# Shift of the maxima in two 64-row tiles, product with v in four 32-column tiles by key tile, and all work in the order of a fixed table

## The chip, the cores and the metric

The kernel runs on one core of a Trainium2 chip. Its engines are TensorE (PE in the profile, its weight loads PEld), VectorE (DVE), ScalarE (ACT), GpSimd (POOL) and SyncE (SP), which issues nearly all DMAs. The metric is the device time of one execution in microseconds (us).

## The reference

Attention with a hash mask over four batches of eight heads, 768 positions and 64 dimensions, and behind it a gated MLP. Cut to what matters:

```python
mask = q_bucket[:, :, :, None] == k_bucket[:, :, None, :]
scores = scale * np.matmul(q, k.transpose(0, 1, 3, 2))
scores = np.where(mask, scores, -1000000000.0)
scores = scores - np.max(scores, axis=-1, keepdims=True)
attn = np.exp(scores)
attn = attn / (np.sum(attn, axis=-1, keepdims=True) + 1e-09)
x = np.matmul(attn, v)            # heads side by side: 4 x 768 x 512

h = gelu(x @ w_in)
u, v = h[..., :512], h[..., 512:]
v_n = (v - mean(v)) / sqrt(var(v) + 1e-6) * g_ln
v_s = einsum('ts,bsd->btd', w_sg, v_n) + b_sg
out = x + (u * v_s) @ w_out
```

## The kernel before, in words

Attention goes by pairs of heads: sixteen pairs, each in two halves of 384 queries, so 32 halves. The two heads of a pair lie in rows 0 to 63 and 64 to 127. For each half PE does this:

- **maxima** (`largest`, L626): the scores of 128 queries against 384 keys, two heads side by side in two tiles of 64 rows, into a pair of PSUM banks. VectorE takes the maximum of each row (L631).
- **shift** (`shift`, L644): the maxima, one per query, are turned from a column into a row by three matmuls against the identity, each with 128 rows, and ScalarE copies two single rows of the result (L650) into row 0 of each head's half of the feature tile, so that the next scores come out with the maximum already taken off.
- **scores** (`weigh`, L666): by key tile of 128 keys, four products of both heads (eight matmuls in tiles of 64 rows) into a pair of banks. ScalarE takes the exponential (L671) into `p`, and GpSimd adds the `p` up (L680).
- **sums** (`total`, L720): four matmuls in tiles of 32 columns add up the rows of the half before ("owed"), and in every second half `project` (L580) makes the features of a later pair in the same tiles.
- **product with v** (`weighted`, L696): for each of six key tiles, two matmuls, one per head, in tiles of 64 columns. They are fp32 and run as two records each, so that a half has twelve rounds of two. ScalarE copies the result out (L711).

PSUM has eight banks; maxima, scores and transposes (L548) take a pair at a time, sums, projection, product and shift one bank each. The MLP of the four batches follows: hidden layer (L892, L923, and L1031 from the second batch on), gate (L1097), output projection (L1126), all in tiles of 128 by 128.

The order is a planner's. Each piece of work is added to `Plan` with an engine, a cost, a priority and what it reads and writes; `Plan.order` replays these costs and always takes the piece that can start first, priorities deciding among equals. It also chooses the PSUM banks. A whole product with v (six key tiles) is one piece there, and so waits for all six `p`. `run` then issues all pieces in that order, and each engine works through its own in program order.

Of the kernel before, what the change touches and what calls it, by code (L numbers as in the profile page):

```python
# [56 lines left out]
SHAPE = {"A": [-0.98, -2.55, -0.98, -3.44, -0.98, -5.54, -0.98, -3.31, -0.98, -0.98, -4.35, -0.98, -2.56, -0.98, -0.98, -0.98, -0.98, -3.67, -0.98, -0.98], "AV": [0.04, 0.0], "C": [3.53, 5.01, 6.13, 6.3], "E": [-0.97, -1.77, -2.62, -1.21, 0.19, -0.97, -1.6, 1.54, -0.61, 3.21, -2.11, -0.97], "M": [0.0, 0.0, 0.0, 0.0, -0.75, -0.2, 0.0, 0.0, 0.0, -0.91, -0.03, -1.94], "R": [2.1, 0.6, 3.9, 0.6, -0.6, 0.6, 0.6, 0.44, 0.6, 1.18, -2.15, 0.6], "S": [1.85, 0.9], "T": [0.55, 0.68], "W": [0.0, 0.0, 0.0, 0.0, 0.0, 0.0, 0.0, 0.0, 0.0, 0.0, 0.0, 0.0], "hi": [3.01, -3.43], "lo": [-0.31, -1.87], "m": [5.85, -3.2], "rc": [-3.79, 1.95], "sm": [2.31, 3.12], "un": [4.14, 8.61], "xt": [6.41, 0.14], "F": [1.92], "sg": [-6.6], "x": [1.49, 1.82]}  # L57


class Plan:  # L60
# [81 lines left out]
    def order(self):  # L142
        G = self.groups
        users = [[] for _ in G]
        need = [0] * len(G)
        for g in G:
            for d in g["deps"] | g["after"]:
                users[d].append(g["n"])
                need[g["n"]] += 1
        at = [0.0] * len(G)  # L150
        wants = [[b for b in g["slots"] if b.first == g["n"]] for g in G]
        left = {}
        for g in G:
            for b in g["slots"]:
                left[b] = left.get(b, 0) + 1
        free, seq, ready, dma_free, pe, till, lanes = {}, {}, {}, 0.0, {0: 1.8, 1: 0.9}, {}, []
        port, form = {"DVE": 0.0, "POOL": 0.0}, None

        def since(n):
            e = G[n]["e"]  # L160
            if G[n]["dma"]:
                return max(seq.get(e, 0.0), lanes[-self.LANES] if len(lanes) >= self.LANES else 0.0)
            return max(free[e], seq.get(e, 0.0), port[e] if G[n]["port"] and not G[n]["dma"] else 0.0)

        def when(n):

            bs = wants[n]
            if len(bs) < 2:
                return max([at[n]] + [min(b.slots.values()) if b.width == 1 else self.place(b)[0] for b in bs])
            s, old, t = bs[0].slots, dict(bs[0].slots), at[n]  # L170
            for b in bs:
                t0, i = self.place(b) if b.width == 2 else min((x, i) for i, x in s.items())
                t = max(t, t0)
                for j in range(i, i + b.width):
                    s[j] = 1e9
            s.update(old)
            return t

        for g in G:
            ready.setdefault(g["e"], [])  # L180
            free.setdefault(g["e"], 0.0)
            if not need[g["n"]]:
                ready[g["e"]].append(g["n"])
        out, at_end = [], {}
        while len(out) < len(G):

            first = {}
            for e, rs in ready.items():
                ws = [n for n in rs if wants[n]]
                if len(ws) > 1:  # L190
                    t = min(max(when(n), since(n)) for n in rs)
                    m = min((n for n in ws if max(at[n], since(n)) <= t + 1e-9), key=lambda n: (G[n]["p"], n), default=None)
                    if m is not None:
                        first[e] = m

            def early(n):
                e = G[n]["e"]
                return not wants[n] or e not in first or first[e] == n

            t0, e = min((max(when(n), since(n)), e) for e, rs in ready.items() for n in rs if early(n))  # L200
            if t0 > 1e8:
                raise RuntimeError("no slot becomes free")
            n = min((n for n in ready[e] if early(n) and max(when(n), since(n)) <= t0 + 1e-9), key=lambda n: (G[n]["p"], n))
            g = G[n]
            soon = [m for m in ready[e] if early(m) and max(when(m), since(m)) <= t0 + self.SOON * g["c"] and (G[m]["p"], m) < (g["p"], n)]
            if soon:
                n = min(soon, key=lambda m: (G[m]["p"], m))
                g = G[n]
            ready[e].remove(n)
            start = max(t0, when(n), since(n))  # L210
            cost = g["c"]
            if e == "PE":

                one, two_ = g["form"] if isinstance(g["form"], tuple) else (g["form"],) * 2
                work = g["c"] + (self.TURN_PE[one] if one != form else 0.0)
                form = two_
                at_, cost = start, 0.0
                while work > 1e-9:

                    k = int(at_ / self.TICK + 1e-9)  # L220
                    slow = 2.0 if pe.get(k - 1, 0.0) < self.WARM * self.TICK else 1.0
                    t = min(work * slow, (k + 1) * self.TICK - at_)
                    pe[k] = pe.get(k, 0.0) + t / slow
                    work, at_, cost = work - t / slow, at_ + t, cost + t
            end, seq[e] = start + cost, start
            if g["dma"] and g["c"] > 1:
                end = dma_free = max(dma_free, start + 0.6) + self.TURN
                seq[e] = max(start + 3.6, end - 1.5)
                end += 0.3
                lanes.append(end + self.WAIT)  # L230
            elif g["lat"]:

                seq[e], end = end, start + g["lat"]
                lanes.append(end + self.WAIT)
            elif g["dma"]:
                seq[e] = end
                end = dma_free = max(dma_free, start + (1.38 if e == "ACT" else 1.3 if g["c"] > 1 else 1.2)) + g["dma"]
                end += 0.75
                lanes.append(end + self.WAIT)
            else:  # L240
                free[e] = end
                if g["port"]:
                    if e == "POOL":
                        port["DVE"] = end - self.LOCK_DVE
                    else:
                        port["POOL"] = end - self.LOCK_POOL
            out.append((start, n))
            at_end[n] = end
            for b in wants[n]:
                b.i = self.place(b, start)[1]  # L250
                for i in range(b.i, b.i + b.width):
                    b.slots[i] = 1e9
            for b in g["slots"]:
# [5 lines left out]
            for m in users[n]:  # L259
# [5 lines left out]
                if not need[m]:  # L265
                    ready[G[m]["e"]].append(m)
# [12 lines left out]
def kernel(  # L279
# [19 lines left out]
    P = 128  # L299
# [892 lines left out]
```

## Time and profile before

| what | value |
|---|---|
| median of three runs | 721.92 us (720.22 to 721.97) |
| the profiled execution's span | 719.5 us |
| PE busy | 709.6 us, 99% |
| PEld / DVE / POOL / ACT busy | 558.0 / 566.4 / 485.7 / 400.2 us |
| product with v, L696 | 768 records, 131.2 us busy |
| shift, L644 | 96 records |

The span is what the profiled execution took from its first instruction to its last; its own time on the device isn't given apart from it, and the runs lie 0.7 to 2.5 us above the span. Busy time of PE counts a matmul from its start to its modelled end, and matmuls overlap, so "99%" says that PE has hardly a pause, not that its array is full: what a stretch of PE work costs is read from the starts of the instructions in it.

### The profile page before, as it was taken

How to read it: one execution, taken by the hardware profiler on the slowest of the kernel's cores; microseconds unless marked ns; L12 is line 12 of the kernel's file. 1: busy time of each engine (PE TensorE's matmuls, PEld its weight loads, DVE VectorE, ACT ScalarE, POOL GpSimd, SP SyncE). 2: the span in 40 equal slices, each digit the busy share in tenths (PEclk: the TensorE clock that was granted, in tenths of full speed). 3: DMA queues.
4: the chain of work that ended last, by engine and by line, in shares of the span. 5: the costliest groups of instructions: out<-in, count | busy, mean ns of one | idle time of the engine just before them, and what ended most of it. 6: DMA issues, size and time to landing. Idle time of an engine off the chain costs nothing.

```text
span 719.5 us, 14177 instructions
## 1 busy us (share of the span) xinstructions
PE 709.6 (99%) x5258; PEld 558.0 (78%) x5258; DVE 566.4 (79%) x830; ACT 400.2 (56%) x645; POOL 485.7 (68%) x322
## 2 busy tenths in 40 slices
PE   8999999999999999999999999999999999999997
PEld 4676776766767676676767669997899889988996
DVE  6987789788988887888889449686698498839963
ACT  2676666657657657665765547522575265425630
POOL 4678788787877867587677848475884847484340
PEclk9999999999999999999999999999999999999999
DMA  6333643663665456256442225915531542244004
GB/s 131 86 62 95 153 112 92 138 134 105 139 131 128 106 120 141 55 139 155 107 123 57 75 86 147 230 34 142 115 96 41 137 88 89 66 111 88 1 1 117
DMA packets 181028, 75.08 MB, mean 104 GB/s; under 512 B 157920, under 2 KB 171232, under 8 KB 180960
## 3 DMA queue, kind: packets, MB, share of 16 engines
q1 hardware_dynamic: 179728, 73.33, 41.9%
q10 hardware_dynamic: 1232, 0.86, 0.4%
q8 instruction: 41, 0.67, 0.4%
q14 instruction: 27, 0.22, 0.1%
HBM read 56.33 MB, written 17.24 MB: 102 GB/s over the span
## 4 chain that ended last, share of the span: by engine, by line
PE 88%; DVE 7%; issue 2%; DMA 2%; ACT 1%; SPq 0%; DVEq 0%; ACTq 0%
PE psb L666 18%; PE psb L696 16%; PE psb L1097 13%; PE psb L892 9%; PE psb L626 8%; PE psb L1126 7%; PE psb L1031 6%; PE psb L548 3%; DVE mx L631 3%; PE psb L923 2%; PE psb L720 2%; PE psb L580 1%; PE psb L644 1%; DMA sq<-s 1%; DVE u L947 1%
## 5 line engine op out<-in xcount | busy, mean ns | idle before, releaser
L680 POOL TENSOR_TENSOR sum<-sum,p 128x768 f32<-128x768 f32 x128 | 224.4, 1753 | 82.5 <-ACT p L671 74.7
L631 DVE TENSOR_REDUCE mx<-psb 128x2 f32<-128x768 f32 x192 | 175.8, 950 | 39.5 <-PE psb L626 37.5
L671 ACT ACTIVATE p<-psb 128x768 f32<-128x768 f32 x192 | 148.9, 814 | 30.7 <-PE psb L666 22.5
L696 PE MATMUL psb<-p,v 128*64 128x385 f32 x768 | 131.2, 491 | 0.0
L696 PEld LDWEIGHTS psb<-p,v 128*64 128x64 f32 x768 | 52.3, 137 | 71.7 <-issue 62.7
L666 PE MATMUL psb<-hq,hk 64*128 64x384 f32 x384 | 72.0, 371 | 1.3 <-ACT p L671 0.7
L680 POOL TENSOR_TENSOR sum<-p,p 128x768 f32<-128x768 f32 x32 | 60.5, 1892 | 11.7 <-ACT p L671 11.5
L626 PE MATMUL psb<-fk,fq 64*128 64x384 f32 x384 | 66.6, 343 | 1.6 <-DVE mx L631 1.0
L1108 POOL TENSOR_TENSOR gs<-gt,gs 128x384 fp32r<-128x384 f32 x32 | 37.6, 1189 | 41.6 <-ACT gs L1105 38.5
L626 PE MATMUL psb<-hk,hq 64*128 64x384 f32 x384 | 64.8, 334 | 0.0
L666 PE MATMUL psb<-hq,lk 64*128 64x384 f32 x384 | 64.7, 333 | 0.0
L666 PE MATMUL psb<-lq,hk 64*128 64x384 f32 x384 | 64.6, 333 | 0.0
L666 PE MATMUL psb<-fq,fk 64*128 64x384 f32 x384 | 64.6, 333 | 0.0
L1097 PE MATMUL psb<-wgh,zh 128*128 128x384 f32 x192 | 64.3, 335 | 0.0
L1097 PE MATMUL psb<-wgh,zl 128*128 128x384 f32 x192 | 64.2, 334 | 0.0
L1097 PE MATMUL psb<-wgl,zh 128*128 128x384 f32 x192 | 64.2, 334 | 0.0
L711 ACT COPY un<-psb 128x385 f32<-128x385 f32 x32 | 15.4, 481 | 84.4 <-PE psb L696 84.4
L1126 PE MATMUL psb<-woh,gs 128*128 128x512 f32 x192 | 60.3, 391 | 0.2 <-DVE gt L1100 0.2
L908 POOL TENSOR_TENSOR zl<-y,zh 128x512 fp32r<-128x512 f32 x24 | 33.0, 1374 | 29.6 <-ACT zh L907 26.1
L666 PEld LDWEIGHTS psb<-hq,hk 64*128 64x128 f32 x384 | 36.0, 184 | 13.0 <-DVE mx L631 5.2
L1126 PEld LDWEIGHTS psb<-woh,gs 128*128 128x128 f32 x192 | 36.1, 188 | 8.2 <-DVE gt L1100 0.6
L626 PEld LDWEIGHTS psb<-fk,fq 64*128 64x128 f32 x384 | 36.0, 184 | 7.1 <-DVE mx L631 3.8
(157 smaller groups left out, 1584.8 us busy)
## 6 DMA issues: line engine op xcount, KB each, us to landing
q<-in_q_dram SPq DMA_DIRECT2D x32, 192.0 KB, 4.2
v<-in_v_dram SPq DMA_DIRECT2D x16, 384.0 KB, 3.9
rs<-r SPq DMA_DIRECT2D x64, 96.0 KB, 3.1
xs<-xt SPq DMA_DIRECT2D x32, 192.0 KB, 4.0
xl<-xs SPq DMA_DIRECT2D x16, 384.0 KB, 4.5
rx<-xs SPq DMA_DIRECT2D x96, 64.0 KB, 2.4
out_dram<-ob SPq DMA_DIRECT2D x24, 256.0 KB, 2.3
k<-in_k_dram SPq DMA_DIRECT2D x31, 192.0 KB, 4.4
```

The source lines that it names most:

```text
L626: nc.tensor.matmul(sc[kh]()[:, j, :SH], x[0]()[row(j), qs], x[1]()[row(j), kh * SH:(kh + 1) * SH], start=(n == 0), stop=(n == 1))
L631: plan.add(DVE, 0.95, prio + OM[2 * t + kh], lambda kh=kh: nc.vector.tensor_reduce(mx()[:, i, :, kh], sc[kh]()[:, :, :SH], axis=AX.X, op=A ...
L666: nc.tensor.matmul(sc[i]()[:, j, :SH], x()[row(j), ks], y()[row(j), cs], start=(n == 0), stop=(n == 3))
L671: plan.add(ACT, 0.81, prio, lambda i=i: nc.scalar.activation(p[i]()[:, :, :SH], sc[i]()[:, :, :SH], AF.Exp), [sc[i]], [p[i], ticks[-1]], t ...
L680: plan.add(POOL, 1.88, prio + 0.6, lambda i=i, first=first: nc.gpsimd.tensor_add(sums(), (first or sums)()[:, :, :SH], p[i]()[:, :, :SH]), ...
L696: nc.tensor.matmul(av()[row(j), :SH + 1], v_()[:, j, kt, :], p[kt]()[:, j, :], start=(kt == 0), stop=(kt == NT - 1))
L892: nc.tensor.matmul(ps(), x()[:, ts_], w[:, c, FH:FF], start=(c == 0 and n == 0), stop=(c == NC - 1 and n == 2))
L908: plan.add(POOL, 1.35, p0, lambda y=y, t=t: nc.gpsimd.tensor_sub(zl()[:, t, :], y(), zh()[:, t, :].bitcast(F32)), [y, (zh, t)], [(zl, t)])
L1031: nc.tensor.matmul(ps()[:, :SH], a()[:, c, fs], y[c](), start=(c == 0 and n == 0), stop=(c == HC - 1 and n == 2))
L1097: nc.tensor.matmul(vp()[:, :SH], z()[:, t, fs], w()[:, t, cs], start=(t == 0 and n == 0), stop=(t == NT - 1 and n == 2))
L1108: nc.gpsimd if e == POOL else nc.vector).tensor_sub(gl()[:, cs], gt(), gh()[:, cs].bitcast(F32)),
L1126: nc.tensor.matmul(po(), a()[:, ts_], w()[:, f, :], start=(f == 0 and n == 0), stop=(f == NF - 1 and n == 2))
```

## The change

Four things change. The shift is made in two tiles of 64 rows, so six matmuls of 64 columns each into a pair of banks, and its two copies on ScalarE gather the 384 values from both banks. The product with v is made in four tiles of 32 columns (two heads, two halves of the head's dimensions), and each key tile is a piece of its own, which waits for its own `p` alone. The sums no longer wait for the last `p`. And `order` no longer plans: it returns a table of the numbers of all pieces, with a second table for the banks.

```diff
+ORDER = [
+    2, 0, 3, 1, 4, 6, 5, 7, 8, 16, 20, 10, 9, 18, 12, 17, 11, 14, 13, 15, 40, 19, 21, 41, 42, 22, 48, 44, 43, 50, 23, 45, 58, 24, 49, 39, 46, 47, 25, 51,
...
+BANKS = [
+    0, 2, 4, 6, 4, 4, 0, 0, 2, 6, 6, 4, 0, 4, 6, 2, 2, 0, 2, 6, 4, 2, 6, 0, 4, 0, 6, 0, 6, 2, 6, 6, 0, 2, 4, 2, 0, 4, 4, 2,
...
     def order(self):
-        G = self.groups
-        users = [[] for _ in G]
...
-        return [n for _, n in sorted(out, key=lambda x: x[0])]
+        banks = iter(BANKS)
+        for g in self.groups:
+            for b in dict.fromkeys(g["slots"]):
+                if b.first == g["n"]:
+                    b.i = next(banks)
+        assert sorted(ORDER) == list(range(len(self.groups)))
+        return ORDER
...
-            mx, m, tp = st.mx, plan.buf("m", len(msts), lambda i: msts[i % len(msts)]), ps_one()
+            mx, m, tp = st.mx, plan.buf("m", len(msts), lambda i: msts[i % len(msts)]), ps_two()
...
                 for i in range(HT):
-                    nc.tensor.matmul(tp()[:W, i * P:(i + 1) * P], m()[:, i, :W], identr, start=True, stop=True)
-
-            plan.add(PE, 0.18, prio, spread, [m], [tp], tag="S")
+                    for j in range(2):
+                        nc.tensor.matmul(tp()[:W, j, i * D:(i + 1) * D], m()[row(j), i, :W], identr[row(j), row(j)], start=True, stop=True)
+
+            plan.add(PE, 0.25, prio, spread, [m], [tp], form="row", tag="S")
...
-                plan.add(ACT, 0.47, prio, lambda r=r: nc.scalar.copy(ft()[r:r + 1, cs], tp()[r:r + 1, :SH]), [tp], [(ft, hf)], tag="C")
+                plan.add(ACT, 0.47, prio, lambda r=r: nc.scalar.copy(
+                    ft()[r:r + 1, cs].rearrange("a (i j c) -> a j i c", i=HT, j=2),
+                    tp()[r:r + 1, :, :HT * D].rearrange("a j (i c) -> a j i c", i=HT)), [tp], [(ft, hf)], tag="C")
...
-            def product():
-                for kt in range(NT):
-                    for j in range(2):
-                        nc.tensor.matmul(av()[row(j), :SH + 1], v_()[:, j, kt, :], p[kt]()[:, j, :], start=(kt == 0), stop=(kt == NT - 1))
-
-            if owed is None:
-                plan.add(PE, 1.3 * HT, prio, product, p + [v_], [av], form="col")
-            else:
+            def product(kt):
+                for j in range(2):
+                    for h in range(2):
+                        r, d = j * D + h * Q, slice(h * Q, (h + 1) * Q)
+                        nc.tensor.matmul(av()[r:r + Q, :SH + 1], v_()[:, j, kt, d], p[kt]()[:, j, :], start=(kt == 0), stop=(kt == NT - 1))
+
+            if owed is not None:
...
-                plan.add(PE, 0.35 + (0.66 if nxt else 0.0), prio - 0.02, sumup, p[-1:] + [sums] + (nxt.raw if nxt else []), [tp] + ([nxt.fp] if nxt else []), form="col32")
-                plan.add(PE, 1.3 * HT, prio - 0.01, product, p + [v_], [av], form="col", tag="AV")
+                plan.add(PE, 0.35 + (0.66 if nxt else 0.0), prio - 0.02, sumup, [sums] + (nxt.raw if nxt else []), [tp] + ([nxt.fp] if nxt else []), form="col32")
+            for kt in range(NT):
+                plan.add(PE, 0.65, prio - 0.01 + 0.0001 * kt, lambda kt=kt: product(kt), [p[kt], v_], [av], form="col32", tag="AV")
```

The lines of the changed file stand eight to eleven lower in number: L615 is maxima (L626 before), L634 the shift (L644), L658 the scores (L666), L689 the product with v (L696), L712 the sums (L720), L569 the projection (L580), L884 the hidden layer (L892), L1089 the gate (L1097), L1118 the output projection (L1126).

On PE, the end of a half in the middle of the attention stood so before; `fk`, `fq` are features, `hq` and `lk` the high and low parts of q and k, `mst` the maxima:

```order
L626 MATMUL psb<-hk_5_3132,hq_5_3156 128x384 x2
L720 MATMUL psb<-sum_3151,ones 32x192 x4
L580 MATMUL psb<-q_3207,pw 32x384 x2
L580 MATMUL psb<-k_3186,pw 32x384 x2
L696 MATMUL psb<-p_159,v_2870 64x385 x2
L696 MATMUL psb<-p_160,v_2870 64x385 x2
L696 MATMUL psb<-p_161,v_2870 64x385 x2
L696 MATMUL psb<-p_162,v_2870 64x385 x2
L696 MATMUL psb<-p_163,v_2870 64x385 x2
L696 MATMUL psb<-p_164,v_2870 64x385 x2
L644 MATMUL psb<-identr,mst 66x128 x3
L666 MATMUL psb<-hq_5_3156,hk_5_3132 128x384 x2
```

The same place on PE in the changed program:

```order
L615 MATMUL psb<-hk_5_3407,hq_5_3387 128x384 x2
L712 MATMUL psb<-sum_3397,ones 32x192 x4
L569 MATMUL psb<-q_3498,pw 32x384 x2
L569 MATMUL psb<-k_3524,pw 32x384 x2
L689 MATMUL psb<-p_159,v_3329 32x385 x4
L689 MATMUL psb<-p_160,v_3329 32x385 x4
L689 MATMUL psb<-p_161,v_3329 32x385 x4
L689 MATMUL psb<-p_162,v_3329 32x385 x4
L689 MATMUL psb<-p_163,v_3329 32x385 x4
L689 MATMUL psb<-p_164,v_3329 32x385 x4
L634 MATMUL psb<-identr,mst 66x64 x6
L658 MATMUL psb<-hq_5_3387,hk_5_3407 128x384 x2
```

The pieces stand as they did, but from sums to product the tiles no longer change their shape (32 columns throughout), nor from shift to scores (64 rows). In some halves the product is cut open. On PE, the end of the second pair's first half now reads:

```order
L615 MATMUL psb<-hk_1_999,hq_1_1011 128x384 x2
L689 MATMUL psb<-p_157,v_726 32x385 x4
L712 MATMUL psb<-sum_829,ones 32x192 x4
L615 MATMUL psb<-fk_176,fq_175 128x384 x2
L615 MATMUL psb<-hk_1_999,hq_1_1011 128x384 x2
L615 MATMUL psb<-fk_176,fq_175 128x384 x2
L615 MATMUL psb<-hk_1_999,hq_1_1011 128x384 x2
L689 MATMUL psb<-p_158,v_726 32x385 x4
L689 MATMUL psb<-p_159,v_726 32x385 x4
L689 MATMUL psb<-p_160,v_726 32x385 x4
L634 MATMUL psb<-identr,mst 66x64 x6
L615 MATMUL psb<-fk_176,fq_175 128x384 x2
```

Maxima stand between the key tiles of one product there, and the last two key tiles come behind the shift. Counted over the whole program, PE changes the shape of its tiles 167 times before and 112 times now: from 64 rows to narrow columns 32 times before and 36 times now, from 32 columns to 64 columns 31 times before and never now, from 64 columns to the shift's 128 by 128 31 times before and never now; the transposes' changes stay. Three groups of maxima in a row stand in 17 places before, in 10 now.

In the MLP the blocks are mixed. On PE, the first output projections (L1118) now stand among gate (L1089) and the next batch's hidden layer (L884), where before all 144 matmuls of the gate, all 72 of the projection and all 72 of the hidden layer followed each other:

```order
L1118 MATMUL psb<-woh_6048,gs_6172 128x512
L1118 MATMUL psb<-wol_5972,gs_6172 128x512
L1118 MATMUL psb<-woh_6048,gs_6178 128x512
L1089 MATMUL psb<-wgh_5768,zh_5715 128x384
L1089 MATMUL psb<-wgl_5797,zh_5715 128x384
L1089 MATMUL psb<-wgh_5768,zl_5725 128x384
L884 MATMUL psb<-wih,xh_6072 128x512
L884 MATMUL psb<-wil,xh_6072 128x512
L884 MATMUL psb<-wih,xl_5959 128x512
```

The matmuls themselves are the same ones, with the same tiles; only their sequence is another.

## Rows read from the trace of the kernel before

**Rows 1.** The page: span, busy time of PE, granted clock in forty slices.

```profile
span 719.5 us, 14177 instructions
...
PEclk9999999999999999999999999999999999999999
```

**Rows 2.** Busy time by stretch, attention and MLP (us, instructions in brackets).

```profile
30.00:415.00 385.00, 382.87 (x3530) 269.58 (x3528) 323.21 (x393) 243.61 (x377) 297.18 (x170) 1.00 0.47 112
415.00:720.00 305.00, 299.93 (x1544) 270.24 (x1540) 220.15 (x381) 141.59 (x249) 175.40 (x130) 1.00 0.37 94
```

**Rows 3.** Timeline of PE, end of a half: start us, us, line, operation, count.

```profile
273.12 0.34 PE L626 MATMUL psb<-hk,hq 64*128 64x384 f32 x2
273.38 0.53 PE L720 MATMUL psb<-sum,ones 128*32 128x192 f32 x8
273.74 0.49 PE L580 MATMUL psb<-q,pw 128*32 128x384 f32 x2
...
274.06 0.49 PE L580 MATMUL psb<-q,pw 128*32 128x384 f32 x2
...
274.49 4.10 PE L696 MATMUL psb<-p,v 128*64 128x385 f32 x24
278.52 0.40 PE L644 MATMUL psb<-identr,mst 128*66 128x128 f32 x3
278.85 0.44 PE L666 MATMUL psb<-hq,hk 64*128 64x384 f32 x2
279.13 0.34 PE L666 MATMUL psb<-hq,lk 64*128 64x384 f32 x2
279.31 0.34 PE L666 MATMUL psb<-lq,hk 64*128 64x384 f32 x2
```

**Rows 4.** Timeline of the weight loads in the same stretch.

```profile
274.49 0.20 PEld L696 LDWEIGHTS psb<-p,v 128*64 128x64 f32 x4 [0.62 <-ACT p L671]
274.87 0.14 PEld L696 LDWEIGHTS psb<-p,v 128*64 128x64 f32 x2 [0.18 <-issue]
275.19 0.14 PEld L696 LDWEIGHTS psb<-p,v 128*64 128x64 f32 x2 [0.18 <-issue]
...
277.78 0.14 PEld L696 LDWEIGHTS psb<-p,v 128*64 128x64 f32 x2 [0.18 <-issue]
278.52 0.26 PEld L644 LDWEIGHTS psb<-identr,mst 128*66 128x66 f32 x3 [0.60 <-DVE lq L557]
278.85 0.19 PEld L666 LDWEIGHTS psb<-hq,hk 64*128 64x128 f32 x2
278.96 0.19 PEld L666 LDWEIGHTS psb<-hq,lk 64*128 64x128 f32 x2
```

**Rows 5.** The line of the shift: duration of one, ns (min/median/max).

```profile
L644 PEld LDWEIGHTS psb<-identr,mst x96: 133/138/142, 18.7 to 403.1; 128*66 128x66 f32 x96
```

**Rows 6.** Timeline of PE, the one change from 32 columns to 64 rows.

```profile
20.83 0.49 PE L580 MATMUL psb<-q,pw 128*32 128x384 f32 x2
20.84 0.49 PE L580 MATMUL psb<-k,pw 128*32 128x384 f32 x2
21.26 0.44 PE L666 MATMUL psb<-hq,hk 64*128 64x384 f32 x2
21.55 0.34 PE L666 MATMUL psb<-hq,lk 64*128 64x384 f32 x2
```

**Rows 7.** Waits of weight loads from 21 to 414 us: total, times, longest.

```profile
PEld psb L666 <- DVE mx L631: 5.2, 21, 0.7
PEld psb L666 <- ACT p L671: 3.7, 12, 0.5
PEld psb L626 <- DVE mx L631: 1.3, 4, 0.6
```

**Rows 8.** Waits of PE from 415 us to the end.

```profile
PE psb L892 <- DVE ob L1129: 0.7, 1, 0.7
PE psb L1126 <- DVE gt L1100: 0.2, 1, 0.2
```

**Rows 9.** ScalarE's lines behind product and shift, and the exponential: ns of one.

```profile
L711 ACT COPY un<-psb x32: 463/482/489, 34.9 to 422.1; 128x385 f32<-128x385 f32 x32
L650 ACT CAST fq<-psb x64: 451/469/474, 19.8 to 403.9; 1x384 fp32r<-1x384 f32 x64
L671 ACT ACTIVATE p<-psb x192: 804/814/863, 22.3 to 415.3; 128x768 f32<-128x768 f32 x192
```

More of the change, by code (lines that the diff above doesn't have):

```diff
@@ L142, in order @@
     def order(self):
-        G = self.groups
-        users = [[] for _ in G]
[L145 to L239, printed above, removed]
-            else:
[L241 to L253, printed above, removed]
-                left[b] -= 1
-                till[b] = max(till.get(b, 0), end)
-                if not left[b]:
-                    for i in range(b.i, b.i + b.width):
-                        b.slots[i] = till[b] + self.WAIT
-            for m in users[n]:
-                need[m] -= 1
-                if n in G[m]["deps"]:
-                    at[m] = max(at[m], end if G[m]["e"] == e and not g["dma"] else end + self.WAIT)
-                else:
-                    at[m] = max(at[m], start)
-                if not need[m]:
-                    ready[G[m]["e"]].append(m)
@@ L267, in order @@
-        self.span = max(t for t, _ in out)
-        self.times = {n: (t, at_end[n]) for t, n in out}
-        return [n for _, n in sorted(out, key=lambda x: x[0])]
+        banks = iter(BANKS)
[5 more added lines that the diff above has]
+        return ORDER
     def run(self, tc):
@@ L691, in weighted @@
             half.n, half.b, half.hp, half.hf, half.av, half.sum = st.n, st.b, st.hp, hf, av, st.sum
-            def product():
-                for kt in range(NT):
-                    for j in range(2):
-                        nc.tensor.matmul(av()[row(j), :SH + 1], v_()[:, j, kt, :], p[kt]()[:, j, :], start=(kt == 0), stop=(kt == NT - 1))
-            if owed is None:
-                plan.add(PE, 1.3 * HT, prio, product, p + [v_], [av], form="col")
-            else:
+            def product(kt):
[4 more added lines that the diff above has]
+            if owed is not None:
                 sums, tp = owed.sum, ps_one()
```

101 rows, old and new, of tables (BANKS, ORDER) are left out of this document.

## The prediction

> **What bounds the kernel now.** I read the page first, then busy time by stretch, then the waits, and last the timeline of PE in one half. The page gives a span of 719.5 us and a granted clock at its top, 2.4 GHz, in every slice [rows 1]: nothing is to be had from the clock. By stretch PE is busy 382.87 of 385 us in the attention and 299.93 of 305 in the MLP, while VectorE has 323.21 and 220.15, GpSimd and ScalarE less [rows 2]. So PE's program, one instruction behind the other, sets the end, and the question is what stands between its starts. The waits that the profile names are few: in the attention the largest three make 10.2 us in 37 places [rows 7], and the loads shown there are normally hidden, so that PE itself lost less than that; in the MLP PE waited 0.9 us in two places [rows 8]. The rest is matmuls that stream, and a toll that recurs wherever tiles change their shape. That toll is what the timeline of one half shows [rows 3]; the change acts on just this.
>
> **The product's tiles.** In the product with v a round starts every 0.32 us (274.87, 275.19) [rows 4]. The projection's two rounds, four tiles of 32 columns each with 384 columns to stream, also start 0.32 us apart (273.74, 274.06) [rows 3]. So four narrow tiles stream beside each other as two wider ones do, and twelve rounds stay twelve rounds of 0.32: the doubled number of instructions costs nothing, its loads lie under the running round as they do in L580. What goes is the change from 32 to 64 columns: from the projection's last round to the product's first it is 0.43 us (274.06 to 274.49) instead of 0.32, and from the product's first to its second 0.38 (274.49 to 274.87) instead of 0.32 [rows 3, 4]. That is 0.11 + 0.06 = 0.17 us, in 31 halves (the first half has no sums to be made): **-5.3 us**. Since it is one form throughout, I bound it by -5.3 and by 0 (if the first round of a product is late for a reason of its own).
>
> **The shift.** Before, the last round of the product starts at 277.78 + 0.32 = 278.10, the shift at 278.52, the scores at 278.85 and their second pair at 279.13 [rows 3, 4]: 1.03 us, in which two changes of shape are paid (0.42 instead of 0.32, and 0.28 instead of the 0.18 that pairs of scores otherwise take, 279.13 to 279.31). Now one change remains, from 32 columns to 64 rows. The trace has it once, at the start: 0.43 from the last round of the projection (20.83 to 21.26) and 0.29 to the next pair [rows 6], so 0.11 on either side of the change. The new shift itself is not in the trace. Its three loads before take 0.26 us together, one 0.138 [rows 4, 5], so they follow each other by (0.26 - 0.138) / 2 = 0.06. If the six small matmuls go side by side in three pairs at that step, the sum is 0.43 to the first pair, 0.06 + 0.11 to the second, 0.06 to the third, 0.11 to the scores (the step of their loads, 278.85 to 278.96 [rows 4]) and 0.17 to their second pair: 0.94 us, 0.09 less than before. If they go one by one, it is 0.43 + 0.11 + 5 x 0.06 + 0.11 + 0.17 = 1.12, 0.09 more. If the change costs less behind such small loads (0.06 in place of 0.11, as at the product's first round), it is 0.89, 0.14 less. I take pairs, since maxima and scores in such tiles start in pairs (x2 in one row) [rows 3]: 32 x -0.09 = **-2.9 us**, with ends at -4.5 and +2.9.
>
> The Trainium skill speaks against this part: "TensorEngine Tiling (Array Packing)", section Instruction Overhead, says that a matmul has a fixed cost of about 60 cycles, so that one column takes as long as 60, and that no tiling factor should be taken from a dimension that is already small. By that rule the six matmuls of 64 columns would be hardly shorter each than the three were, and the shift would gain nothing. The step of 0.06 us between loads agrees with a floor of that kind; whether pairs share it no row here shows.
>
> **The order.** PE's program goes from rows of 64 to narrow columns 36 times now instead of 32, because some products are cut open. Each such detour costs an entry (L626 to L720 0.26 instead of 0.18, so 0.08 [rows 3]) and an exit (0.11 + 0.11 [rows 6]), 0.30 us: 4 x 0.30 = **+1.2 us**. The changes into and out of the transposes stay in number.
>
> What the table does to the waits I can only bound. In the attention at most the 10.2 us of rows 7 can vanish. The signs are mild and favourable: three groups of maxima in a row, behind which VectorE (323 of 385 us busy, rows 2) is late most, stand in 10 places instead of 17, and a product may begin before its last `p` is there. In the MLP the mixing can win back no more than the 0.9 us of rows 8 and what hides beside them; PE has the same matmuls to do. I take **-2 us** for both, the small change that few waits allow, and keep -9 and +9 as ends (a wait of the present kind taken away nearly everywhere, or doubled).
>
> Edits that I cost at nothing: the loads for narrow tiles (hidden under a round of 0.32; uncovered they would show as a longer round), the two single-row copies from two banks on ScalarE (0.469 us each [rows 9], ScalarE is busy 244 of 385 us [rows 2]; if they grew by half, scores would be asked for later only where no other work is at hand), and the moved DMAs, on which PE doesn't wait in rows 7 or 8.
>
> **Sum.** -5.3 - 2.9 + 1.2 - 2.0 = -9.0 us on the span, 719.5 to 710.5. The median of the runs lies 2.4 us above the profiled span; with the same distance the time is **712.9 us**. A measurement of this kernel can tell about 0.3% (2.2 us) from no change, so faster means below 719.8 and slower above 724.1.
>
> **Rivals.**
>
> *The small matmuls and the waits eat the gain.* The rule above as a mechanism of this kernel: the shift's six matmuls run one after the other, +2.9 us in place of -2.9, and the waits stay as they are: -5.3 + 2.9 + 1.2 = -1.2, so 720.7, no change to be told. For it: the step of 0.06 that doesn't depend on work hidden elsewhere [rows 5]; against it: pairs in all other rows of that shape [rows 3].
>
> *PSUM after the shift becomes the bound (slower).* The shift takes a pair of banks now. Before, product and shift shared one pair; now, at the end of a half, one pair is held by the product until ScalarE has copied it (0.482 us), and another by the shift until two copies of 0.469 are through, so 0.48 + 0.94 = 1.42 us behind the product's end [rows 9]. PE fills the two free pairs with scores (four steps of 0.17, so 0.69) and maxima (0.35) in 1.04 us after the shift's 0.3, then takes the product's pair, and wants the fourth 0.69 later, at about 2.0. That is enough by 0.6. With one exponential (0.814) queued ahead of the copies on ScalarE it is short by 0.2, with two by 1.0, and the scores behind it wait. It decides from 9.0 / 32 = 0.28 us per half; at 0.5 us it is 16 us, so +7.0 and 728.9. For it: the second bank is real, and PE already waits for `p` in 12 places [rows 7]. Against it: ScalarE is idle while the product runs, 142 of 385 us in all [rows 2], and the copies stand first in its program after the product.
>
> *The four streams get into each other's way.* Two of the four tiles read the same columns of `p`, which the projection's tiles don't. If they took turns, a round would double: 12 x 0.32 x 32 = +123 us. Nothing in the rows speaks for it.
>
> *More waits vanish than I count.* If the table takes away nearly all of rows 7 and 8, the waits give -9 in place of -2, and the shift -4.5: 719.5 - 5.3 - 4.5 + 1.2 - 9 = 701.9, so 704.3.
>
> **How the numbers follow.** My forecast has 0.62, the vanished waits 0.13, the eaten gain 0.14, PSUM 0.10, the streams 0.01. The forecast's own range is 708.5 to 717.5 (shift and waits between halves of their ends). To leave no more than two in ten out, the range reaches towards the fewer waits as far as 707, and on the other side takes in the eaten gain, up to 721. Faster: 0.62 + 0.13 and a third of the eaten gain, 0.80. Same: the rest of that and a tip of PSUM's, 0.10. Slower: 0.10.
>
> **What would show it.** After the change, sums, projection and product should start every 0.32 us without a longer step between them; a step of 0.43 there, or rounds longer than 0.32, would refute the first term. From the last round of a product to the second pair of scores it should be near 0.94 us; 1.03 or more refutes the second. The waits for L631 and L671 by weight loads should not exceed 10 us in the attention; if scores behind the shift wait for L650 or L711, PSUM is what I got wrong. In the MLP PE should have no pause over 1 us. I am wrong altogether if rounds and shift are as I say and the time is still above 720.

## The result, and the profile after

The changed kernel takes 731.57 us (median of 5 runs, 726.91 to 733.28), the kernel before 721.92 (5 runs, 720.22 to 722.20): a ratio of 1.0135, with a 95% interval of 1.0104 to 1.0167. It is slower, where faster was forecast. The profiled execution is the shortest of the five, 726.91 us, so its trace shows 5 of the 9.7 us; the four longer ones had a granted clock of 0.995 to 0.999, the profiled one 1.000, and of them there is no trace.

The page's span and chain of waits, of after and then the chain of before:

```profile
span 725.1 us, 15776 instructions
...
PEclk9999999999999999999999999999999999999999
...
PE 74%; DVE 11%; DMA 8%; issue 3%; ACT 2%; SPq 1%; ACTq 0%; DVEq 0%
```

```profile
PE 88%; DVE 7%; issue 2%; DMA 2%; ACT 1%; SPq 0%; DVEq 0%; ACTq 0%
```

The clock is at its top as before [rows 1]. But where PE made 88% of the chain that set the end, it makes 74% now; VectorE and the DMAs have grown from 9 to 19%.

First the shapes. The timeline of PE at the end of a half that isn't held up, and the weight loads in it (L712 sums, L569 projection, L689 product, L634 shift, L658 scores, L615 maxima):

```profile
169.43 0.49 PE L569 MATMUL psb<-q,pw 128*32 128x384 f32 x2
...
169.75 0.49 PE L569 MATMUL psb<-q,pw 128*32 128x384 f32 x2
...
170.07 4.06 PE L689 MATMUL psb<-p,v 128*32 128x385 f32 x48
174.06 0.36 PE L634 MATMUL psb<-identr,mst 64*66 64x64 f32 x6
174.26 0.42 PE L658 MATMUL psb<-hq,hk 64*128 64x384 f32 x2
174.52 0.34 PE L658 MATMUL psb<-hq,lk 64*128 64x384 f32 x2
```

```profile
169.75 0.13 PEld L689 LDWEIGHTS psb<-p,v 128*32 128x32 f32 x4 [0.19 <-issue]
170.07 0.13 PEld L689 LDWEIGHTS psb<-p,v 128*32 128x32 f32 x4 [0.19 <-issue]
170.40 0.13 PEld L689 LDWEIGHTS psb<-p,v 128*32 128x32 f32 x4 [0.19 <-issue]
...
173.31 0.13 PEld L689 LDWEIGHTS psb<-p,v 128*32 128x32 f32 x4 [0.19 <-issue]
174.06 0.26 PEld L634 LDWEIGHTS psb<-identr,mst 64*66 64x66 f32 x6 [0.63 <-issue]
```

The projection and the product follow each other at 0.32 us (169.43, 169.75, 170.07), and the loads of the product at 0.32 to 0.33; the steps of 0.43 and 0.38 of [rows 3, 4] are gone. From the product's last round (173.31 + 0.32 = 173.63) to the second pair of scores (174.52) it is 0.89 us instead of 1.03. In this half both shapes do what was forecast of them.

Then the waits. PE's own from 21 to 427 us, the attention, without its two smallest rows (before: 2.2 us in all, none over 0.7); the largest of its weight loads' for an engine's result in the same time (before: [rows 7]); and PE's from 427 us on, the MLP (before: [rows 8]):

```profile
PE psb L634 <- DVE mst L628: 6.0, 6, 2.5
PE psb L658 <- DVE mx L620: 2.5, 2, 1.8
PE psb L615 <- ACT p L663: 1.7, 2, 1.3
PE psb L615 <- DMA fk<-fc: 1.4, 3, 0.6
PE psb L615 <- DVE mx L620: 1.2, 3, 0.6
PE psb L634 <- ACT un L703: 0.7, 1, 0.7
```

```profile
PEld psb L634 <- DVE mst L628: 9.8, 9, 3.1
```

```profile
PE psb L1023 <- DVE ob L1121: 1.2, 1, 1.2
PE psb L884 <- DVE ob L1121: 0.7, 1, 0.7
PE psb L1089 <- POOL zl L900: 0.4, 1, 0.4
```

In the attention PE waits 14.1 us where it waited 2.2. The largest part, 6.0 us, is ahead of the shift, for the minimum; no such wait was there before. In the MLP it is 2.3 instead of 0.9 us.

A sum over PE's program says the same. The time from each start to the next, put to the kind of work that the stretch begins with, in us, up to the end of the attention (the setup ahead of it left out; the last two rows count from PE's first start, 1.3 us into the span, to its last). e5 and e8 are experiments below, which keep before's order:

```
                                before   after     e5     e8
projection                        11.4     9.9    9.8    9.8
sums                              13.0    11.0   11.0   11.0
product with v (and what is
 waited ahead of the shift)      129.0   135.3  127.9  128.7
shift                             10.6     6.4   10.6    6.4
maxima                            79.5    80.7   79.8   81.2
scores                           143.1   144.8  144.5  146.0
transposes                        23.9    24.7   23.9   24.6
pieces of the MLP                  3.9     6.5    3.9    3.9
attention ends after             422.4   426.9  419.4  419.2
from there to PE's last start    291.6   292.6  291.2  290.6
```

Projection, sums and shift win 7.7 us. The product's row should win 1.1 more (e5) and is 6.3 worse. What the MLP gave to the attention (2.6 us) it doesn't get back at its end.

How a minimum comes late is seen on VectorE. Its timeline in the changed kernel (L620 takes the maxima, L628 the minimum that the shift needs), PE's and GpSimd's of the same time, and VectorE's at the same work before (L631, L639):

```profile
105.30 0.95 DVE L620 TENSOR_REDUCE mx<-psb 128x2 f32<-128x768 f32 x1
...
106.26 1.19 DVE L393 TENSOR_SCALAR wy<-wx 128x512 int32<-128x512 int32 x1
107.38 1.81 DVE L620 TENSOR_REDUCE mx<-psb 128x2 f32<-128x768 f32 x2
109.11 2.23 DVE L394 SCALAR_TENSOR_TENSOR wy<-w,wy 128x512 f32<-128x512 uint32 x1
111.26 0.16 DVE L628 TENSOR_REDUCE mst<-mx 128x6 fp32r<-128x18 f32 x1
```

```profile
106.25 2.77 PE L689 MATMUL psb<-p,v 128*32 128x385 f32 x32
111.47 0.37 PE L634 MATMUL psb<-identr,mst 64*66 64x64 f32 x6 [2.45 <-DVE mst L628]
```

```profile
108.97 1.81 POOL L672 TENSOR_TENSOR sum<-p,p 128x768 f32<-128x768 f32 x1
```

```profile
107.78 1.78 DVE L631 TENSOR_REDUCE mx<-psb 128x2 f32<-128x768 f32 x2
109.59 0.17 DVE L639 TENSOR_REDUCE mst<-mx 128x6 fp32r<-128x18 f32 x1
109.68 1.31 DVE L404 TENSOR_SCALAR wy<-wx 128x512 int32<-128x512 int32 x1
```

The last maxima are done at 109.19, and before, the minimum follows at once. In the table a weight conversion stands between; it takes 2.23 us, and PE, through with its product at 109.0, stands still until 111.47. Read off the two programs: other work stands between the last maximum and the minimum in 3 of 32 halves before (4 instructions), in 14 after (20).

SP's queue has the like. Its four small DMAs that scatter the features (L600), which the maxima need:

```profile
94.32 0.52 SPq L600 DMA_DIRECT2D fq<-fc  x1
94.93 2.17 SPq L600 DMA_DIRECT2D fk<-fc  x1
97.15 0.58 SPq L521 DMA_DIRECT2D k<-in_k_dram  x1
97.82 0.49 SPq L739 DMA_DIRECT2D xs<-xt  x1
98.40 0.39 SPq L730 DMA_DIRECT2D sq<-s  x1
98.84 0.48 SPq L600 DMA_DIRECT2D fk<-fc  x1
99.37 0.59 SPq L600 DMA_DIRECT2D fq<-fc  x1
```

They take 5.6 us, with three others between; PE's next maxima wait for them (0.64 us at 101.27). Before, 3 of the 15 groups of four were split, with 6 DMAs between; after, all 15, with 77.

### The profile page after: what moved, and what is told of

It reads as the page before. It is cut to its first block, busy times and chain, and to the rows that moved or that the text cites. A ratio compares the mean times of both kernels' runs of the same rounds, so it can differ in the third digit from the quotient of the medians.

```text
span 725.1 us, 15776 instructions
## 1 busy us (share of the span) xinstructions
PE 701.7 (97%) x6122; PEld 554.0 (76%) x6122; DVE 562.5 (78%) x830; ACT 395.5 (55%) x645; POOL 487.9 (67%) x322
## 4 chain that ended last, share of the span: by engine, by line
PE 74%; DVE 11%; DMA 8%; issue 3%; ACT 2%; SPq 1%; ACTq 0%; DVEq 0%
PE psb L658 15%; PE psb L1089 12%; PE psb L689 12%; PE psb L1118 8%; PE psb L615 7%; PE psb L884 7%; PE psb L1023 6%; DVE mx L620 4%; PE psb L537 3%; PE psb L915 2%; DMA rx<-xs 2%; DMA rs<-r 2%; PE psb L712 1%; DMA r<-sq 1%; DMA fk<-fc 1%
## 5 line engine op out<-in xcount | busy, mean ns | idle before, releaser
L672 POOL TENSOR_TENSOR sum<-sum,p 128x768 f32<-128x768 f32 x128 | 232.4, 1821 | 51.1 <-ACT p L663 46.5
L620 DVE TENSOR_REDUCE mx<-psb 128x2 f32<-128x768 f32 x192 | 178.7, 952 | 46.0 <-PE psb L615 42.0
L689 PE MATMUL psb<-p,v 128*32 128x385 f32 x1536 | 133.6, 488 | 0.0
L689 PEld LDWEIGHTS psb<-p,v 128*32 128x32 f32 x1536 | 47.9, 110 | 66.4 <-issue 61.1
L672 POOL TENSOR_TENSOR sum<-p,p 128x768 f32<-128x768 f32 x32 | 63.8, 1994 | 41.5 <-ACT p L663 41.5
L615 PE MATMUL psb<-fk,fq 64*128 64x384 f32 x384 | 70.9, 356 | 5.2 <-DVE mx L620 1.9
L658 PE MATMUL psb<-hq,hk 64*128 64x384 f32 x384 | 70.5, 349 | 2.8 <-DVE mx L620 2.5
L1100 POOL TENSOR_TENSOR gs<-gt,gs 128x384 fp32r<-128x384 f32 x32 | 33.8, 1067 | 49.7 <-ACT gs L1097 40.9
L658 PE MATMUL psb<-lq,hk 64*128 64x384 f32 x384 | 67.0, 332 | 0.0
L658 PE MATMUL psb<-fq,fk 64*128 64x384 f32 x384 | 67.0, 332 | 0.0
L658 PE MATMUL psb<-hq,lk 64*128 64x384 f32 x384 | 67.0, 332 | 0.0
L615 PE MATMUL psb<-hk,hq 64*128 64x384 f32 x384 | 66.6, 333 | 0.0
L1118 PE MATMUL psb<-woh,gs 128*128 128x512 f32 x192 | 65.7, 391 | 0.1
L1089 PE MATMUL psb<-wgh,zl 128*128 128x384 f32 x192 | 64.5, 336 | 0.4 <-POOL zl L900 0.4
L1089 PE MATMUL psb<-wgh,zh 128*128 128x384 f32 x192 | 64.5, 336 | 0.0
L1089 PE MATMUL psb<-wgl,zh 128*128 128x384 f32 x192 | 64.3, 335 | 0.0
L615 PEld LDWEIGHTS psb<-fk,fq 64*128 64x128 f32 x384 | 38.1, 184 | 16.0 <-DVE mx L620 5.5
L658 PEld LDWEIGHTS psb<-hq,hk 64*128 64x128 f32 x384 | 38.3, 184 | 7.7 <-DVE mx L620 3.1
L1118 PEld LDWEIGHTS psb<-woh,gs 128*128 128x128 f32 x192 | 36.0, 188 | 7.7 <-DVE gt L1092 0.4
```

The costliest lines, as they stand in the source:

```text
L615: nc.tensor.matmul(sc[kh]()[:, j, :SH], x[0]()[row(j), qs], x[1]()[row(j), kh * SH:(kh + 1) * SH], start=(n == 0), stop=(n == 1))
L620: plan.add(DVE, 0.95, prio + OM[2 * t + kh], lambda kh=kh: nc.vector.tensor_reduce(mx()[:, i, :, kh], sc[kh]()[:, :, :SH], axis=AX.X, op=A ...
L658: nc.tensor.matmul(sc[i]()[:, j, :SH], x()[row(j), ks], y()[row(j), cs], start=(n == 0), stop=(n == 3))
L672: plan.add(POOL, 1.88, prio + 0.6, lambda i=i, first=first: nc.gpsimd.tensor_add(sums(), (first or sums)()[:, :, :SH], p[i]()[:, :, :SH]), ...
L689: nc.tensor.matmul(av()[r:r + Q, :SH + 1], v_()[:, j, kt, d], p[kt]()[:, j, :], start=(kt == 0), stop=(kt == NT - 1))
L1089: nc.tensor.matmul(vp()[:, :SH], z()[:, t, fs], w()[:, t, cs], start=(t == 0 and n == 0), stop=(t == NT - 1 and n == 2))
```

## The experiments

The letters are theories; each text put in says what they expected. A: the shapes gain, the table's order loses. B: the shapes themselves cost. C: the shapes gain, and any order but before's costs some 8 us. D: the gain can't be kept, since another engine or a DMA takes over. The others are told where they come. Times are medians; each ratio is to runs of the kernel before on the same chip, which gave 720.0 to 720.6.

**The shapes without the table, and the table without the shapes.** e1: before with both shapes, its planner left to order the work (and the product one piece); e2: the product's alone; e3: the changed kernel with the old shapes in the table's order.

```
e1, e2   -  nc.tensor.matmul(av()[row(j), ...], v_()[:, j, kt, :], ...)
         +  for h in range(2): ... matmul(av()[r:r + Q, ...], v_()[:, j, kt, d], ...)
         -  plan.add(PE, 1.3 * HT, ..., product, ..., form="col")
         +  plan.add(PE, 1.3 * HT, ..., product, ..., form="col32")
e1       +  the shift's matmuls as in the change
e3       the same lines of the changed kernel put back to before's
```

> Both new tile shapes (product in four 32-column tiles, shift in two 64-row tiles) under the planner of before, the product as one piece, no table. Theory A (shapes gain what the rows of before say, the table's order makes PE wait): 721.9 - 5.3 - 2.9, so 712 to 716. Theory B (the new shapes themselves cost, by the pair of PSUM banks or slower rounds, and the order is neutral): 724 to 731.

> The product in four 32-column tiles alone, shift as before, planner of before. Theory A: the step from sums to product loses 0.17 us in 31 halves, so about 5 us less than before: 715.5 to 718. Theory B with slower rounds: 722 or more; theory B with the shift's banks as the cost: also 716 to 718, so e1 minus e2 tells.

> The table's order and banks with the shapes of before (product in two 64-column tiles per key tile, shift in three 128-row matmuls). Theory A: the changed kernel's 731.6 plus the 8 us that the shapes gain, and some for products that are cut open: 737 to 742. Theory B: 718 to 724.

Measured: e1 724.18, ratio 1.0057 [1.0045, 1.0069]; e2 725.01, 1.0065 [1.0053, 1.0077]; e3 735.71, 1.0219 [1.0200, 1.0238]. In the table the shapes win: 1.0219 falls to 1.0135, 6 us, and the order with the old shapes costs 2.2%, 15.6 us (A had expected 737 to 742, so a little more; B 718 to 724). That speaks against B. But e1 and e2 missed what A expects and lie where B put them: without the table the shapes don't win either. There the planner, told of the new form, had drawn up another order, which e5 to e8 take apart.

**Two places of the table mended.** e4: minima right behind the last maximum, the four scatter DMAs together; e7: also the `xt` up to three maxima later on VectorE.

```
-  return ORDER
+  for n in [the minima] + [the scatter DMAs]:
+      order.remove(n)
+      order.insert(<right behind the last of those n depends on>, n)
+  (e7) each xt is put behind the maxima that follow it, up to three
```

> The changed kernel with two things moved in its table: the shift's minimum on VectorE stands right behind the last maximum it needs (before weight conversions that stand ahead of it in the table), and the four scatter DMAs of the features stand right behind what they need in the DMA queue. Theory A: of some 16 us that PE waits more, 6.7 are ahead of shifts and about 2 behind scatters; half to most of it goes: 723 to 728. Theory B: 730 to 733, no change.

> e4, and on VectorE each multiplication by the reciprocal (xt), which waits for a DMA, stands up to three maxima later in the table. Theory C in its form for the table (PE waits because VectorE's queue is held by what waits for DMAs and by other work ahead of maxima): 2 to 5 us less than e4, ratio 1.001 to 1.006. Rival (the table's waits have another cause, such as PSUM): as e4, 1.006 to 1.011.

Measured: e4 725.87, 1.0082 [1.0054, 1.0110], as A expects: 4 us (by the ratios) to 6 us (by the medians) back. e7 729.96, 1.0151 [1.0125, 1.0177]: a third place mended takes them away again, against the expectation; why was not looked into.

**The order held fixed.** e5: before with the product's new tiles alone, every engine's sequence and all banks as before (one loop changed, costs and forms not told to the planner). e6: e2's order with the old tiles. e8: both shapes in before's sequence; only the PSUM banks are dealt anew, so that a shift gets a pair where one is free.

> Only the product's tiles change (four of 32 columns); the planner decides as before, so that every engine's sequence, every bank and every DMA stand as in the kernel before. Theory C (shapes gain what was predicted, and any other order than the old one makes PE wait some 8 us more, which is what e1 and e2 lost): 5 us less than before, ratio 0.991 to 0.995. Rival D (the gain cannot be had, since another engine takes over as soon as PE is faster): 0.998 to 1.003.

> The planner's order of e2 with the product in the two 64-column tiles of before: another order alone, not one instruction more or less. Theory C: e2 plus 5 us, ratio 1.011 to 1.016. Rival D: the order is as good as the old one, ratio 0.998 to 1.004.

> Both new shapes in the sequence of before: every engine's order is that of the kernel before, only the PSUM banks are dealt out again so that each shift has a pair. Theory C: 8 us less than before, ratio 0.986 to 0.991. Rival D: 0.998 to 1.003. If the pair of banks is what costs: between e5 and 1.005.

Measured: e5 721.31 (717.83 to 722.72, 11 runs), 1.0009 [0.9996, 1.0022]; e6 728.84, 1.0124 [1.0103, 1.0146]; e8 717.55 (716.73 to 720.00, 10 runs), 0.9971 [0.9960, 0.9982]. e6 against e2 shows the product's tiles to win 0.6% in one order, which alone costs 1.2%. e8 is faster than both kernels, and as it lies below e5, the shift's pair of banks costs nothing that shows. But C expected 0.991 to 0.995 of e5 and 0.986 to 0.991 of e8: e5 lies in D's range, e8 just below it. (e5's profiled execution, at 717.83, lies 3.5 us below its median, so its column above is its best case.) The table above tells where the rest went: in e8 projection, sums, product and shift win 8.1 us, and maxima, scores and transposes, with the same instructions in the same order, give 5.3 back.

**What gives it back.** In e8 VectorE stands idle for the sums that come back through DRAM, ahead of their reciprocals, with maxima queued behind them; it did so before (the second line), but for less:

```profile
DVE sq L787 <- DMA sq<-s: 23.0, 14, 5.1
```

```profile
DVE sq L739 <- DMA sq<-s: 17.9, 12, 4.7
```

That is the form of D that e9 to e12 test; E says that maxima and exponentials set the pace themselves. e9 is e8 with reciprocals of a tile of ones, so that the division by the sums is left out, e10 the same of before; e11 is e8 with the reciprocals moved later, e12 the same of before.

```
e9, e10    -  V.reciprocal(sq(), sq())
           +  V.reciprocal(sr, ones[:, :W6])
           -  eng.dma_start(rd..., sq())
           +  eng.dma_start(rd..., sr)
e11, e12   +  each reciprocal behind the maxima and minima that follow it, up to three
```

> Both shapes in before's order (as in the run before), but the reciprocals on VectorE are taken of a tile of ones and not of the sums that come back through DRAM, so VectorE waits for no DMA there; this leaves the division by the sums out. All instructions and DMAs stay and stand in the same order. With the sums VectorE stood idle 23.0 us in 14 places ahead of its reciprocals, with maxima queued behind. Theory D (the shapes' gain is given back because VectorE, held up by the DMA of the sums, brings maxima and minima late): at least 3 us less than 717.6, so 714.5 or less, ratio 0.990 to 0.992. Theory E (maxima and exponentials themselves set the pace, PE only catches up with them): 716.5 to 718.5, as with the sums.

> The control for the run above: the kernel before, with reciprocals of ones (the division by the sums is left out), same order. Theory D: PE is late enough there to hide the wait, so less than 1.5 us is won, 718.5 to 720. If it wins as much as the kernel with both shapes does (3 us or more), the wait cost the same before and doesn't explain where the shapes' gain went.

> Both shapes in before's order, sums divided by as always, but each reciprocal is moved on VectorE's queue behind the next one to three maxima and minima, where these follow at once. Theory D: some of the wait is covered, 715 to 717, 0.5 to 2.5 us less than 717.6. Theory E: no gain, 717 to 719, since maxima came no earlier than PE asked; and if the later reciprocals make the DMAs behind them late, slower, 719 to 723.

> The control for the run above: the kernel before with the reciprocals moved in the same way. Theory D: 719 to 720.5, within 1 us of before, since PE seldom waited for maxima there. Theory E: the same. Slower by over 2 us would show that the later reciprocals cost something of their own through the DMAs behind them.

Measured: e9 716.78, 0.9946 [0.9929, 0.9964]; e10 720.50, 1.0000 [0.9985, 1.0014]; e11 722.06, 1.0026 [1.0008, 1.0044]; e12 725.22, 1.0071 [1.0046, 1.0096]. e9 wins 0.25% on e8 (the two intervals overlap by a little) and e10 nothing: the wait is worth something, if at all, only once PE is faster. By its time e9 lies in E's range and above D's. The waits of VectorE and PE in e9 show where some of the idle time went:

```profile
DVE xt L796 <- DMA rs<-r: 11.5, 3, 4.5
```

```profile
PE psb L660 <- ACT p L718: 2.2, 2, 1.5
PE psb L713 <- DVE mx L665: 2.0, 3, 1.4
```

VectorE now stands idle at the next link of the chain, ahead of `xt`, in three places (1.0 us in one place in e8). Behind the one at 170.46 it has no gap until 183, and in that stretch PE loses 1.5 us (to `p`) and 1.4 (to maxima); that the one brought about the other isn't shown. D, in this form, doesn't explain the 5.3 us, and E isn't shown by it. In e11 and e12, both slower than D and E have it (the case that the texts named besides), SP's queue tells of a cost of the move itself: with a reciprocal late, its store is late (4.3 us in the rows below), and the features that stand behind it in the queue (2.5 us). PE waits 2.2 us for `fk` in e12, where it waited for none before. SP in e12, and at the same work before:

```profile
70.48 0.33 SPq L755 DMA_DIRECT2D r<-sq  x1
...
73.48 2.26 SPq L625 DMA_DIRECT2D fq<-fc  x2
```

```profile
66.14 0.33 SPq L741 DMA_DIRECT2D r<-sq  x1
...
70.95 1.15 SPq L611 DMA_DIRECT2D fq<-fc  x2
```

**One place of the table at a time.** F: the minima's and the scatter DMAs' places cost by themselves; G: only in an order that is bad already. e13 and e14 put them into before, as often as the table has them; e15 and e16 take them out of the table singly.

```
e13   +  each minimum behind the weight conversion that follows it on VectorE
e14   +  the last two of four scatter DMAs behind the next 3 and 5 DMAs of SP
e15   +  in the table: the minima right behind the last maximum
e16   +  in the table: the four scatter DMAs together
```

> The kernel before, both old shapes, with one thing of the table put in: on VectorE the minimum goes behind the weight conversion that follows it, where one does. Then 16 of the 32 minima have other work between the last maximum and themselves (20 instructions), where before has 3 (4 instructions) and the table 14 (20 instructions). No other queue is changed. Theory F (the place of the minimum on VectorE is a cause of the table's loss; the shift waited 6.0 us for it in 6 places): slower by 3 to 7 us, 723 to 727. Rival G (these places only cost where PE's own order is already bad): within 1.5 us of before.

> The kernel before, both old shapes, with the other thing of the table put in: on SP's queue the last two of the four small DMAs that scatter the features go behind three and five of the DMAs that follow them, never past their first user. All 15 groups of four are then split, with 78 other DMAs between them; before has 3 split groups with 6, the table 15 with 77. No other queue is changed. Theory F: maxima wait for them, slower by 1 to 5 us, 721 to 725. Rival G: within 1.5 us of before.

> The changed kernel with only the minimum moved on VectorE, to right behind the last maximum, in all 32 halves; the scatter DMAs stay as the table has them. Both moves together gave 725.9 instead of 731.6. Theory F: 726.5 to 729.5, 2 to 5 us less than the changed kernel. Rival G: within 1.5 us of 731.6, and both moves are needed.

> The changed kernel with only the four scatter DMAs moved together on SP's queue, to right behind the features they carry; the minimum stays as the table has it. Theory F: 727 to 731, 1 to 4 us less than the changed kernel. Rival G: within 1.5 us of 731.6.

Measured: e13 723.99, 1.0052 [1.0037, 1.0066]; e14 803.36, 1.1148 [1.1126, 1.1169]; e15 729.90, 1.0137 [1.0106, 1.0168]; e16 728.31, 1.0118 [1.0090, 1.0147]. PE's largest waits, of e13 and of e14, one of SP's queue in e14 (L773 loads `v`, L656 is the shift), and PE's busy time in e14:

```profile
PE psb L656 <- DVE mst L651: 5.4, 8, 1.1
```

```profile
PE psb L638 <- issue: 26.0, 9, 4.6
PE psb L638 <- DMA fk<-fc: 23.9, 17, 3.4
```

```profile
SPq L773 <- PE psb L656: 18.8, 14, 1.7
```

```profile
PE 739.8 (92%) x5258; PEld 586.4 (73%) x5258; DVE 557.8 (70%) x830; ACT 401.8 (50%) x645; POOL 480.8 (60%) x322
```

e13 makes the wait ahead of the shift (5.4 us, 6.0 in the changed kernel) out of that one place, and costs 3.7 us, as F expects. e14 loses 83 us, over 16 times what F expected at most, 5.5 us for each of 15 groups: the scatter DMAs now stand, among others, behind a load of `v` that waits for PE to reach the shift, while PE's maxima behind that shift need the scatter. Not all of it is waiting: PE is busy 739.8 us instead of 709.6, since in 69 us of this run the granted clock is at the lower of its two levels (1.2 GHz). So it is from 94.5 to 97.9 us, after PE had idled 2.59 us up to 92.94 and 1.11 up to 94.67, and a pair of scores there takes 0.32 us (95.45 to 95.77) instead of 0.17. What a split costs hangs on what it is put behind; the table's places are less bad ones. e15 and e16 don't decide between F and G: by its time e16 lies in F's range and e15 in neither, and by the ratios one place alone gives nothing that can be told from the changed kernel (1.0135; its runs spread by 6 us), while both together do (e4).

## Why the prediction was wrong

The sum had -8.2 us for the shapes and -0.8 for the order (detours and waits together). e3 parts them: the order costs 15.6 us with the old shapes, and the shapes win 6 us of it back. The last sign of the prediction came true: rounds and shift are as it says, and the time is above 720. So it is the order's term that failed, and in it the waits.

*The product's tiles, -5.3: right for the rows that it was read from.* e5 against before: 1.6 in the projection, 2.0 in the sums, 1.1 in the product, so -4.7. But e5's time didn't fall (1.0009): that a gain in these rows is a gain of the span was wrong in before's order.

*The shift, -2.9: right in kind, larger in size.* In before's order it is 0.90 us instead of 1.03 in 26 of 30 halves (e8), and the shift's row gives -4.2, near the end of -4.5 that I had kept. By the rule that I set against it (the Trainium skill, "TensorEngine Tiling (Array Packing)", section Instruction Overhead, a fixed cost of about 60 cycles, no tiling factor from a small dimension) six matmuls of 64 columns would have won nothing; here six take 0.20 us to the scores (174.06 to 174.26) where three took 0.33 [rows 3], and their starts lie 28 ns apart on the mean instead of 87, so the two row tiles share the step, and the measurement decides. The step of 0.06 us between the old loads, which I took to agree with the rule, is 144 cycles at 2.4 GHz, over twice its 60, and was no sign of it.

*The detours, +1.2:* not measured alone.

*The waits, -2: the step that failed.* I had bounded them by "a wait of the present kind taken away nearly everywhere, or doubled". With the shapes at -8.8 (e5's product and after's own rows) and the span 5.6 longer, all else costs 14.4 us in the profiled execution, and some 18.5 in the medians (9.7 + 8.8); e3 has 15.6, detours included. All are outside the bound. The largest wait that came was none of the present kind: 6.0 us for the minimum, ahead of the shift; waits for maxima grew as well (2.5 us ahead of the scores). I had argued from PE's own order ("three groups of maxima in a row" in 10 places instead of 17), while in the order of VectorE and SP 14 minima stood behind other work instead of 3, and 15 groups were split instead of 3. e13 shows the first to cost 3.7 us by itself in before's order, e4 both to be worth 4 to 6 in the table.

*Moved DMAs "on which PE doesn't wait in rows 7 or 8", costed at nothing: failed too.* That PE hadn't waited for them told only of where they stood. PE waits 1.4 us for `fk` itself, and VectorE's maxima behind it. In the MLP VectorE waits for a load that was mostly early enough before (2.2 us in 2 places); what that cost PE isn't shown:

```profile
DVE ob L1114 <- DMA rx<-xs: 17.3, 8, 5.9
```

*The rivals.* PSUM was the only one on the slow side, and named the wrong mechanism: PE waits 0.9 us for `un` and nowhere for the shift's copies (0.2 before). The eaten gain isn't it, as the shapes' own rows give all that was said. A rival that I lacked is that the gain can't all be kept: in the old order (e8) 5.3 of 8.1 us go back. That a faster PE comes nearer to VectorE, ScalarE and the DMAs, which it doesn't shorten, is my reading of it, not shown: e9 took the largest such wait for a DMA away and won 0.25%. Nor does it hold in every order: e2 against e6 keeps 0.6% of the tiles' 0.65%, and the changed kernel against e3 0.8%.

*What stays open.* 4.7 us of the changed kernel lie between its profiled execution and its median, and where e8 gives 5.3 us back is known by rows but not by cause. And e4's two places leave 0.8% over before, though the shapes win: the rest of the table's cost is spread over places that I didn't take apart, and e7, e11 and e12 show that mending by hand can lose as well.

## What to carry to other kernels

When a change deals out an order anew, read the queues of the engines that feed the bound one, not its own: count, before and after, what stands between the last instruction that feeds a needed result and the one that makes it, and what a small urgent DMA is queued behind. Where PE is 88% of the chain and VectorE is busy for 323 of 385 us [rows 2], a gain on PE is an upper end, not a forecast: in the old order a quarter of it was kept (e8, 0.3% of 1.1%); two slower orders kept more of it, but cost more than the shapes give. Try new shapes in the old order first, and the new order with the old shapes; the two questions are then apart.

## What the runs showed of the hardware

The same weight conversion on VectorE (L394) takes 0.68 us at least and 2.30 at most, with a median of 1.21 (before, as L405, 0.68 to 2.36 with a median of 0.69):

```profile
L394 DVE SCALAR_TENSOR_TENSOR wy<-w,wy x12: 680/1209/2301, 44.3 to 402.1; 128x512 f32<-128x512 uint32 x12
```

At 109.11 it overlaps GpSimd's addition, which ends at 110.78; from there it is 0.56 us to its end, while maxima keep to 0.91 to 0.96 throughout. The Trainium skill, "SBUF — State Buffer", section Who interferes with whom, has it that a VectorE instruction with two inputs in SBUF contends with a GpSimd instruction that reads SBUF, for a pair of ports that only one of them holds at a time, and that a reduction never does; the trace agrees, as far as GpSimd's rough spans can tell. So the price of an instruction put ahead of the minimum was not its 0.7 us, but up to some three times that.
